# Both layers of an MLP block beside the attention of the next batch, with loads reordered and a shorter way for the first decay rows

## The chip, the cores and the metric

The kernel runs on one core of one Trainium2 chip. The metric is the time of one execution in device microseconds (us). Before the change the median was 400.74 us over 3 runs (398.77 to 401.0); a fourth joined later, so the result below has 400.87. A profile is one execution with the hardware profiler on. Its span, from the first instruction to the last, is 1.7 us shorter than the time of that same execution (397.3 of 399.01 us before the change), so spans are compared with spans and times with times.

Engine names in profile lines: PE is the matrix engine, PEld its weight loads, DVE the vector engine, ACT the scalar engine, POOL the GpSimd engine, SP the engine that issues most of the transfers. A name with a q (SPq, ACTq) is an engine's queue of instructions such as DMA issues. A line of the timeline gives start and length in us, engine, source line, operation, tiles, shape and count; a bracket at its end gives how long the engine stood idle before it, and what ended that. The tiles: `qkf` and `v_f` are loaded q, k and v, `t` the cast q and k, `pT` and `pX` transposes, `S` a bank of scores, `Pm` their exponentials, `ph` and `po` the banks of layers 1 and 2, `trl` and `gT` the two steps of the gate, `osb` the output on its way to DRAM. SBUF is the memory on the core that the engines work in; PSUM is the memory that PE writes to, in banks. The granted clock is the share of its full clock that PE was given.

## The reference

Eight batches of eight heads, 576 tokens, head size 64. A causal attention with a decay is followed by a two-layer MLP with a gate:

```python
s_pos = np.maximum(s, 0.0)
cum   = np.cumsum(s_pos, axis=-1)
bias  = -(cum[:, :, :, None] - cum[:, :, None, :])
scores = np.where(causal, -1e9, q @ k.T / 8 + np.minimum(bias, 0.0))
x = softmax(scores) @ v                      # (4608, 512) after the heads are put side by side
h = x @ w_in                                 # layer 1, 512 -> 2048
g = h * np.clip(h + 3.0, 0.0, 6.0) / 6.0     # the gate
out = g @ w_out                              # layer 2, 2048 -> 512
```

## The kernel before

Heads are handled in 32 pairs, four pairs to a batch. A pair's q and k are loaded in f32, cast to f16 on POOL, and transposed on PE in two groups of 5 and 4 tiles; DVE copies each group from PSUM into `qT` and `kT`. Rows 64 to 67 of these hold the decay, so that one matmul gives score plus bias. They come from a scratch tensor in DRAM:

```python
nc.scalar.dma_start(out=kaug_dram..., in_=kaug)     # store all heads' decay rows
nc.scalar.dma_start(out=qaug_dram..., in_=qaug)
load_aug(0, nc.scalar)                              # reload those of pairs 0 and 1
load_aug(1, nc.scalar)
```

The scores of one head are four PSUM banks (tag S, three buffers). ACT makes the exponentials, POOL cuts off the upper triangle, PE multiplies by v (`attend`) and transposes the result into `xT`:

```python
def att_tasks(p):                                   # pair p; the number is the task's cost in the weave
    tasks = [(loads, 0)]                            # aug of p+2, q,k,v of p+3, weights.get(p)
    tasks += 4 x (scores_bank(2p, bi), 400)
    tasks += (attend(2p-1), 1200)
    tasks += (transpose_group(p+1, 0), 640)         # the two groups stand apart
    tasks += 4 x (scores_bank(2p+1, bi), 400)
    tasks += (casts, 0)                             # cast_v(p+1), cast_qk(p+2)
    tasks += (x_transpose(p-1), 640)
    tasks += (transpose_group(p+1, 1), 512)
    tasks += (attend(2p), 1200)
```

*(The additions stand here for the loops and appends of the source.)*

`weave` lays the attention tasks of one batch between the MLP tasks of a block, in proportion to these costs. The MLP works in nine blocks of 512 tokens. One task of layer 1 is four matmuls into a bank, then ACT and DVE make the gate; one task of layer 2 is four of the sixteen matmuls of an output tile:

```python
def m1(n, f):
    ph = psum.tile([128, 512], F32, tag="M", bufs=2)
    ... 4 matmuls ...
    nc.scalar.activation(out=trl, in_=ph, func=AF.Relu, bias=bias3[:, 0:1], scale=1.0)
    nc.vector.scalar_tensor_tensor(out=gT[n][:, f, :], in0=trl, scalar=6.0, in1=ph, ...)

def m2(n, t4, part):
    if part == 0:
        pouts[n, t4] = psum.tile([128, 512], F32, tag="Y", bufs=1, ...)   # one bank
    ... 4 matmuls; after part 3: DVE scales into osb, sync stores it ...

weave(att_of[1], m1_tasks(0))
for n in range(NBLK - 1):                           # layer 1 of n+1 with layer 2 of n, interleaved
    att = att_of[n + 2] if n + 2 < B else []
    weave(att, merged(m1_tasks(n + 1), m2_tasks(n)))
for task in m2_tasks(NBLK - 1):                     # the last layer 2, alone
    task()
```

The weights come in eight chunks on POOL's queue, issued with the loads of pairs 1 to 5: `w_in` with pairs 1 to 3 (two chunks with pair 2), `w_out` with pairs 4 and 5 (two each).

The softmax here doesn't subtract the row's maximum and nothing guards it: scores larger than these inputs give would overflow.

## Time and profile before

| | before |
|---|---|
| median of timed runs | 400.74 us |
| span of the profile | 397.3 us |
| first matmul of layer 1 | 45.0 us |
| end of the stretch with layer 1 of block 0 and batch 1 | 82.6 us |
| a block with both layers and one batch | 39.8 us |
| the last layer 2 with its store | 20.7 us |

### The profile page before, as it was taken

The numbers are of one execution on the slowest core, as the hardware profiler recorded it, in microseconds if no ns is written. First come the engines' busy times: TensorE is split into PE (matmuls) and PEld (weight loads), VectorE is DVE, ScalarE is ACT, GpSimd is POOL, SyncE is SP. The second block draws the span as 40 slices with busy tenths as digits, with TensorE's granted clock in tenths as the row PEclk, the third lists the DMA queues.
The fourth block names the chain that finished last, engine by engine and source line by source line (L and its number), as shares of the span: only waits on it lengthen the run. The fifth ranks groups of instructions, "written<-read, shape, count | busy, mean of one in ns | idle before, by whom it ended". The sixth has DMA issues, their size and how long they took to land.

```text
span 397.3 us, 8194 instructions
## 1 busy us (share of the span) xinstructions
PE 366.4 (92%) x3040; PEld 209.7 (53%) x3040; DVE 227.2 (57%) x417; ACT 210.8 (53%) x406; POOL 140.3 (35%) x333
## 2 busy tenths in 40 slices
PE   7584776899999999999999999999999999999985
PEld 3363443555555555555555555555555544444432
DVE  4574372756666666666666666666665564454511
ACT  6364473755555566666666555555556633443400
POOL 3394825544444444444444444444443200000000
PEclk9999698999999999999999999999999999999999
DMA  9999999955555555554555455455100001010111
GB/s 176 201 213 205 185 208 178 194 108 118 116 118 118 119 117 118 119 117 117 118 118 118 108 126 114 109 126 116 38 28 27 28 26 54 26 53 28 49 58 54
DMA packets 123512, 43.40 MB, mean 109 GB/s; under 512 B 114192, under 2 KB 118672, under 8 KB 123472
## 3 DMA queue, kind: packets, MB, share of 16 engines
q1 hardware_dynamic: 117456, 37.89, 43.9%
q0 software_dynamic: 4224, 4.19, 6.4%
q10 hardware_dynamic: 1792, 0.79, 0.9%
q8 instruction: 24, 0.39, 0.4%
q14 instruction: 16, 0.13, 0.1%
HBM read 37.32 MB, written 9.73 MB: 118 GB/s over the span
## 4 chain that ended last, share of the span: by engine, by line
PE 80%; DMA 10%; POOL 4%; DVE 3%; ACT 2%; issue 1%; SPq 0%; POOLq 0%; ACTq 0%
PE po L335 31%; PE ph L317 29%; PE S L211 8%; DMA qkf<-in_k_dram 7%; PE O L260 6%; PE pT L171 3%; PE pX L285 2%; POOL Pm L224 2%; POOL t L153 1%; DMA kaug_scratch<-kaug 1%; DMA kT<-kaug_scratch 1%; ACT trl L325 1%; ACT Pm L219 1%; DMA s_sb<-in_s_dram 1%; DVE osb L344 1%; DVE gT L326 1%
## 5 line engine op out<-in xcount | busy, mean ns | idle before, releaser
L326 DVE SCALAR_TENSOR_TENSOR gT<-trl,ph 128x512 f16<-128x512 f32 x144 | 98.8, 687 | 114.7 <-ACT trl L325 114.5
L219 ACT ACTIVATE Pm<-S 128x384 f16<-128x384 f32 (+2 forms) x256 | 113.7, 506 | 80.3 <-PE S L211 72.5
L317 PE MATMUL ph<-xT,w_in_sb 128*128 128x512 f16 x576 | 147.4, 381 | 0.0
L335 PE MATMUL po<-w_out_sb,gT 128*128 128x512 f16 x576 | 144.4, 379 | 2.3 <-DVE osb L344 2.3
L325 ACT ACTIVATE trl<-ph,bias 128x512 f32<-128x512 f32 x144 | 99.6, 692 | 82.8 <-PE ph L317 81.0
L224 POOL TENSOR_SCALAR_AFFINE_SELECT Pm<-Pm 128x128 f16<-128x128 f16 (+2 forms) x256 | 78.8, 313 | 154.6 <-ACT Pm L219 144.8
L211 PE MATMUL S<-qT,kT 128*128 128x320 f16 (+4 forms) x448 | 71.4, 265 | 8.0 <-DMA kT<-kaug_scratch 3.0
L335 PEld LDWEIGHTS <-gT 128*128 128x128 f16 x576 | 51.2, 98 | 49.4 <-issue 3.2
L317 PEld LDWEIGHTS <-w_in_sb 128*128 128x128 f16 x576 | 52.2, 98 | 44.5 <-issue 1.1
L211 PEld LDWEIGHTS <-kT 128*128 128x128 f16 x448 | 42.1, 99 | 35.3 <-issue 4.9
L153 POOL CAST t<-qkf 128x1152 f16<-128x1152 f32 x32 | 36.7, 1147 | 21.4 <-DMA qkf<-in_k_dram 21.4
L260 PEld LDWEIGHTS <-Pm 128*128 128x128 f16 x960 | 37.4, 97 | 7.8 <-POOL Pm L224 1.6
L260 PE MATMUL O<-v_h,Pm 128*128 128x65 f16 x960 | 40.8, 193 | 0.5 <-POOL Pm L224 0.5
L171 PE MATMUL pT<-ident,t 128*128 128x128 f16 x288 | 26.8, 222 | 13.5 <-POOL t L153 12.9
L181 DVE COPY qT<-pT 64x640 f16<-64x640 f16 x64 | 28.3, 442 | 17.7 <-PE pT L171 17.6
L171 PEld LDWEIGHTS <-t 128*128 128x128 f16 x288 | 21.1, 99 | 28.1 <-POOL t L153 14.6
L344 DVE TENSOR_SCALAR osb<-po 128x512 f32<-128x512 f32 x36 | 24.8, 690 | 13.8 <-PE po L335 13.2
L182 DVE COPY kT<-pT 64x640 f16<-64x640 f16 x64 | 29.4, 459 | 0.9
L272 DVE TENSOR_TENSOR xs<-O,r 128x640 f16<-128x640 f32 x32 | 26.4, 824 | 1.1
L159 POOL CAST v_h<-v_f 128x640 f16<-128x640 f32 x28 | 20.1, 718 | 0.0
L285 PEld LDWEIGHTS <-xs 128*128 128x128 f16 x160 | 11.8, 99 | 10.9 <-issue 6.2
L293 DVE COPY xT<-pX 128x576 f16<-128x576 f16 x32 | 14.5, 453 | 1.7 <-PE pX L285 1.5
(29 smaller groups left out, 56.6 us busy)
## 6 DMA issues: line engine op xcount, KB each, us to landing
qkf<-in_q_dram SPq DMA_DIRECT2D x32, 288.0 KB
qkf<-in_k_dram SPq DMA_DIRECT2D x32, 288.0 KB
out_dram<-osb SPq DMA_DIRECT2D x36, 256.0 KB
v_f<-in_v_dram SPq DMA_DIRECT2D x62, 128.0 KB
w_in_sb<-in_moe_w_in_dram POOLq DMA_DIRECT2D x4, 512.0 KB, 8.1
w_out_sb<-in_moe_w_out_dram POOLq DMA_DIRECT2D x4, 512.0 KB, 10.1
v_f<-in_v_dram SPq DMA_DIRECT2D x31, 32.0 KB
kT<-kaug_scratch SPq DMA_DIRECT2D x30, 6.8 KB
```

The costliest lines, as they stand in the source:

```text
L153: nc.gpsimd.tensor_copy(out=t, in_=qk_f.pop(p))
L171: nc.tensor.matmul(out=pT[:, (t - t0) * 128:(t - t0 + 1) * 128], lhsT=src[:, t, :, :], rhs=ident, is_transpose=True, start=(t == t0), stop ...
L182: nc.vector.tensor_copy(out=kT[0:64, sl, c0:c0 + n], in_=pT[64:128, 0:n])
L211: nc.tensor.matmul(out=S[:, c:c + hi - lo], lhsT=kT[:, sl, off + 128 * kt:off + 128 * (kt + 1)], rhs=qT[:, sl, off + lo:off + hi], start=( ...
L219: nc.scalar.activation(out=P[:, p0:p0 + n], in_=S[:, 0:n], func=AF.Exp, scale=0.125, bias=0.0)
L224: nc.gpsimd.affine_select(out=view, in_=view, pattern=pattern, compare_op=ALU.is_ge, fill=0.0, base=0, channel_multiplier=-1,)
L260: nc.tensor.matmul(out=O[:, hh, qt * VW:qt * VW + D + 1], lhsT=P[:, c:c + 128], rhs=v_h[:, sl, hh, kt, 0:D + 1], start=(qt == 0), stop=(qt ...
L317: nc.tensor.matmul(out=ph, lhsT=w_in_sb[:, kc, f * 128:(f + 1) * 128], rhs=xT[:, kc, n * 512:(n + 1) * 512], start=(kc == 0), stop=(kc == ...
L325: nc.scalar.activation(out=trl, in_=ph, func=AF.Relu, bias=bias3[:, 0:1], scale=1.0)
L326: nc.vector.scalar_tensor_tensor(out=gT[n][:, f, :], in0=trl, scalar=6.0, in1=ph, op0=ALU.min, op1=ALU.mult)
L335: nc.tensor.matmul(out=po, lhsT=gT[n][:, f, t4 * 128:(t4 + 1) * 128], rhs=w_out_sb[:, f, :], start=(f == 0), stop=(f == NF - 1),)
L344: nc.vector.tensor_scalar_mul(out=osb, in0=po, scalar1=1.0 / 6.0)
```

## The change

Five things are changed together. Both layers of block n now run in turn beside the attention of batch n+1, layer 1 with a small share of the attention and layer 2 with most of it; so block 0 is finished beside batch 1 and the last layer 2 no longer stands alone after its own layer 1. The layer-2 bank joins the banks of layer 1 (three buffers for both). From pair 4 on, both transpose groups of the next pair stand together at the end of a pair, with the cast right before `attend`. Loads and weight chunks are issued in order of need. Pair 0's decay rows go straight from SBUF to SBUF instead of through DRAM. Two small edits come along: v of pair 0 is loaded from SP's queue instead of ACT's, and PE gets fewer warm-up matmuls at the start (18 and 6 instead of 22 and 10). The diff, cut to its core:

```diff
-        ph = psum.tile([128, 512], F32, tag="M", bufs=2)
+        ph = psum.tile([128, 512], F32, tag="M", bufs=3)
...
-            pouts[n, t4] = psum.tile([128, 512], F32, tag="Y", bufs=1, name=f"po{n}_{t4}")
+            pouts[n, t4] = psum.tile([128, 512], F32, tag="M", bufs=3, name=f"po{n}_{t4}")
...
     mask_rows(0, nc.scalar.copy)
+    for r in range(2):
+        for hh in range(2):
+            nc.scalar.dma_start(
+                out=kT[64 + r:65 + r, 0, hh * SEQ:(hh + 1) * SEQ], in_=kaug[hh:hh + 1, r, :]
+            )
     nc.scalar.activation(out=qaug, in_=c8, func=AF.Copy, scale=-1.0)
-    mask_rows(1, nc.scalar.copy)
+    for hh in range(2):
+        c0, c1 = hh * SEQ, (hh + 1) * SEQ
+        nc.scalar.dma_start(out=qT[67:68, 0, c0:c1], in_=qaug[hh:hh + 1, :])
+        nc.scalar.dma_start(out=kT[66:67, 0, c0:c1], in_=kaug[hh:hh + 1, 2, :])
     ... the two stores to DRAM ...
-    load_aug(0, nc.scalar)
+    mask_rows(1, nc.scalar.copy)
     load_aug(1, nc.scalar)
...
+    loads_at = {0: [3], 1: [4]}             # pairs 5 and 6: see `late`; from pair 5 on: p + 2
+    weights_at = {1: 0, 2: 1, 3: 2, 4: 3}   # w_in chunks
...  att_tasks, for p >= 4
+            if more:
+                c.append((lambda: cast_qk(p + 1), 0))
+            c.append((lambda: attend(2 * p), 1200))
+            c.append((casts, 0))
+            if more:
+                c.append((lambda: transpose_group(p + 1, 0), 640))
+                c.append((lambda: transpose_group(p + 1, 1), 512))
...
+    def block_tasks(n, w1):                 # w1: weight of a layer-1 task against 1.0 of layer 2
+        ts = [(lambda f=f: m1(n, f), w1) for f in range(NF)]
+        ts += [(lambda t4=t4, part=part: m2(n, t4, part), 1.0 if 4 * t4 + part < 13 else 0.0) ...]
...
+    late = {                                # issued after that task of block 0
+        1: lambda: load_w_out(0),
+        4: lambda: load_w_out(1),
+        7: lambda: (load_qk(5, nc.sync), load_v(5, nc.sync), load_w_out(2)),
+        10: lambda: load_w_out(3),
+        13: lambda: (load_qk(6, nc.sync), load_v(6, nc.sync)),
+    }
...
-    weave(att_of[1], m1_tasks(0))
-    for n in range(NBLK - 1):
-        att = att_of[n + 2] if n + 2 < B else []
-        weave(att, merged(m1_tasks(n + 1), m2_tasks(n)))
-    for task in m2_tasks(NBLK - 1):
-        task()
+    weave(att_of[1], first)
+    for n in range(1, NBLK):
+        weave(att_of[n + 1] if n + 1 < B else [], block_tasks(n, 0.3))
```

More of the change, by code (lines that the diff above doesn't have):

```diff
@@ L161, in banks @@
     def banks(early):
-        return dict(tag="M", bufs=2) if early else dict(tag="S", bufs=3)
+        return dict(tag="M", bufs=3) if early else dict(tag="S", bufs=3)
     def transpose_group(p, g):
@@ L349, with keep_warm @@
     nc.vector.memset(bias3, 3.0)
+    def keep_warm(n):
+        pw = psum.tile([128, 512], F32, tag="M", bufs=3, name="pw")
+        for i in range(n):
+            nc.tensor.matmul(
+                out=pw, lhsT=warm[:, 0:128], rhs=warm, start=(i == 0), stop=(i == n - 1)
+            )
     load_qk(0, nc.sync)
-    load_v(0, nc.scalar)
     load_qk(1, nc.sync)
+    load_v(0, nc.sync)
     load_v(1, nc.sync)
@@ L358 @@
     mask_rows(0, nc.scalar.copy)
+    for r in range(2):
+        for hh in range(2):
+            nc.scalar.dma_start(
+                out=kT[64 + r:65 + r, 0, hh * SEQ:(hh + 1) * SEQ], in_=kaug[hh:hh + 1, r, :]
+            )
     nc.scalar.activation(out=qaug, in_=c8, func=AF.Copy, scale=-1.0)
-    mask_rows(1, nc.scalar.copy)
+    for hh in range(2):
+        c0, c1 = hh * SEQ, (hh + 1) * SEQ
+        nc.scalar.dma_start(out=qT[67:68, 0, c0:c1], in_=qaug[hh:hh + 1, :])
+        nc.scalar.dma_start(out=kT[66:67, 0, c0:c1], in_=kaug[hh:hh + 1, 2, :])
     nc.scalar.dma_start(
@@ L364, with loads @@
     nc.scalar.dma_start(out=qaug_dram.rearrange("r (h t) -> h (r t)", h=NH), in_=qaug)
-    load_aug(0, nc.scalar)
+    mask_rows(1, nc.scalar.copy)
     load_aug(1, nc.scalar)
-    def keep_warm(n):
-        pw = psum.tile([128, 512], F32, tag="M", bufs=2, name="pw")
-        for i in range(n):
-            nc.tensor.matmul(
-                out=pw, lhsT=warm[:, 0:128], rhs=warm, start=(i == 0), stop=(i == n - 1)
-            )
-    weights = {
-        1: [(load_w_in, 0)],
-        2: [(load_w_in, 1), (load_w_in, 2)],
-        3: [(load_w_in, 3)],
-        4: [(load_w_out, 0), (load_w_out, 1)],
-        5: [(load_w_out, 2), (load_w_out, 3)],
-    }
-    def att_tasks(p):
-        def loads():
-            if p + 2 < NP:
-                load_aug(p + 2, nc.sync)
-            if p + 3 < NP:
-                load_qk(p + 3, nc.sync)
-                load_v(p + 3, nc.sync)
-            for load, c in weights.get(p, []):
-                load(c)
-        more = p + 1 < NP
-        tasks = [(loads, 0)]
-        for bi in range(4):
-            tasks.append((lambda bi=bi: scores_bank(2 * p, bi), 400))
-        if p > 0:
-            tasks.append((lambda: attend(2 * p - 1), 1200))
-        if more:
-            tasks.append((lambda: transpose_group(p + 1, 0), 640))
-        for bi in range(4):
-            tasks.append((lambda bi=bi: scores_bank(2 * p + 1, bi), 400))
+    loads_at = {0: [3], 1: [4]}
+    weights_at = {1: 0, 2: 1, 3: 2, 4: 3}
+    def loads(p):
+        if p + 2 < NP:
+            load_aug(p + 2, nc.sync)
+        for m in loads_at.get(p, [p + 2] if 5 <= p < NP - 2 else []):
+            load_qk(m, nc.sync)
+            load_v(m, nc.sync)
+        if p in weights_at:
+            load_w_in(weights_at[p])
+    def att_tasks(p):
+        more = p + 1 < NP
+        early = p < 4
         def casts():
@@ L409, in casts @@
                 cast_v(p + 1)
-            if p + 2 < NP:
+            if early and p + 2 <= 4:
                 cast_qk(p + 2)
-        tasks.append((casts, 0))
+        a = [(lambda: loads(p), 0)]
+        for bi in range(4):
+            a.append((lambda bi=bi: scores_bank(2 * p, bi), 400))
         if p > 0:
-            tasks.append((lambda: x_transpose(p - 1), 640))
-        if more:
-            tasks.append((lambda: transpose_group(p + 1, 1), 512))
-        tasks.append((lambda: attend(2 * p), 1200))
-        return tasks
+            a.append((lambda: attend(2 * p - 1), 1200))
+        if early:
+            a.append((lambda: transpose_group(p + 1, 0), 640))
+        for bi in range(4):
+            a.append((lambda bi=bi: scores_bank(2 * p + 1, bi), 400))
+        if early:
+            a.append((casts, 0))
+        if p > 0:
+            a.append((lambda: x_transpose(p - 1), 640))
+        c = []
+        if early:
+            c.append((lambda: transpose_group(p + 1, 1), 512))
+            c.append((lambda: attend(2 * p), 1200))
+        else:
+            if more:
+                c.append((lambda: cast_qk(p + 1), 0))
+            c.append((lambda: attend(2 * p), 1200))
+            c.append((casts, 0))
+            if more:
+                c.append((lambda: transpose_group(p + 1, 0), 640))
+                c.append((lambda: transpose_group(p + 1, 1), 512))
+        return a, c
+    att_of = [[]]
+    for p in range(NP):
+        a, c = att_tasks(p)
+        att_of[-1] += a
+        if p % 4 == 0 and p > 0:
+            att_of.append([])
+        att_of[-1] += c
+    att_of[-1] += [(lambda: attend(NH - 1), 1200), (lambda: x_transpose(NP - 1), 640)]
     def weave(att, mlp):
         total = float(sum(c for _, c in att)) or 1.0
-        done = 0.0
-        for i, task in enumerate(mlp):
-            while att and done / total < i / len(mlp):
+        whole = float(sum(w for _, w in mlp))
+        done, due = 0.0, 0.0
+        for task, w in mlp:
+            due += w
+            while att and done / total < due / whole:
                 a, c = att.pop(0)
@@ L432, in weave @@
             a()
-    def m1_tasks(n):
-        return [lambda f=f: m1(n, f) for f in range(NF)]
-    def m2_tasks(n):
-        return [lambda t4=t4, part=part: m2(n, t4, part) for t4 in range(4) for part in range(4)]
-    def merged(a, b):
-        out_ = []
-        for t in range(4):
-            f, g = a[4 * t:4 * t + 4], b[4 * t:4 * t + 4]
-            out_ += [g[0], g[1], f[0], g[2], f[1], g[3], f[2], f[3]]
-        return out_
-    keep_warm(22)
+    def block_tasks(n, w1):
+        ts = [(lambda f=f: m1(n, f), w1) for f in range(NF)]
+        ts += [
+            (lambda t4=t4, part=part: m2(n, t4, part), 1.0 if 4 * t4 + part < 13 else 0.0)
+            for t4 in range(4) for part in range(4)
+        ]
+        return ts
+    keep_warm(18)
     cast_qk(0)
@@ L454 @@
     cast_qk(1)
-    keep_warm(10)
-    att_all = []
-    cut = []
-    for b in range(B):
-        for p in range(4 * b, 4 * b + 4):
-            att_all += att_tasks(p)
-            if p % 4 == 0:
-                cut.append(len(att_all) - 2)
-    att_all += [(lambda: attend(NH - 1), 1200), (lambda: x_transpose(NP - 1), 640)]
-    cut.append(len(att_all))
-    att_of = [att_all[cut[b]:cut[b + 1]] for b in range(B)]
-    for task, _ in att_all[:cut[1]]:
-        task()
-    weave(att_of[1], m1_tasks(0))
-    for n in range(NBLK - 1):
-        att = att_of[n + 2] if n + 2 < B else []
-        weave(att, merged(m1_tasks(n + 1), m2_tasks(n)))
-    for task in m2_tasks(NBLK - 1):
-        task()
+    keep_warm(6)
+    for task, _ in att_of[0]:
+        task()
+    first = block_tasks(0, 0.2)
+    first[:8] = [(task, 0.0) for task, _ in first[:8]]
+    late = {
[5 more added lines that the diff above has]
+    }
+    for i, what in late.items():
+        task, w = first[i]
+        first[i] = ((lambda task=task, what=what: (task(), what())), w)
+    weave(att_of[1], first)
+    for n in range(1, NBLK):
+        weave(att_of[n + 1] if n + 1 < B else [], block_tasks(n, 0.3))
 _INS = ['q', 'k', 'v', 's', 'moe_w_in', 'moe_w_out']
```

## The prediction

> **What bounds the kernel now.** I read three views in this order: the busy time in stretches of the span, the chain that ended last, and the timeline where the two said something. First the stretches (start:end, their sum, busy us of PE, PEld, DVE, ACT, POOL with instruction counts, granted clock, DMA share, GB/s):
>
> ```profile
> 30.00:40.00 10.00, 4.51 (x74) 3.66 (x73) 4.70 (x10) 4.63 (x12) 3.77 (x10) 0.95 1.17 206
> 40.00:50.00 10.00, 7.37 (x70) 4.93 (x71) 3.93 (x9) 4.84 (x10) 8.86 (x18) 0.71 1.05 183
> 50.00:60.00 10.00, 7.22 (x76) 4.47 (x74) 7.06 (x13) 6.78 (x14) 2.26 (x7) 1.00 1.21 208
> ...
> 100.00:120.00 20.00, 20.00 (x182) 11.85 (x181) 12.73 (x25) 12.04 (x24) 8.48 (x20) 1.00 0.54 116
> ```
>
> There are two regimes. Until about 80 us the DMA engines are full (share 1.0, near 200 GB/s) and PE has gaps. From 90 us to 380 us PE is busy for the whole of every stretch and nothing else is near full. The chain names what PE waited for early on (start, length):
>
> ```profile
> 29.03 11.91 DMA qkf<-in_k_dram
> ...
> 45.22 16.20 DMA qkf<-in_k_dram
> ```
>
> These are the loads of pairs 5 and 7, stretched because the weight chunks move beside them.
>
> PE prices, as distances between starts in the timeline: a 128x512 matmul 0.216 us (8 in 1.73); the 15 of one attend 0.47; transposes of a pair 0.28 + 0.23; the x transposes 0.28; four score banks of a head 0.38 + 0.31. A pair of heads is then 2x0.69 + 2x0.47 + 0.79 = 3.11 us, a batch of four pairs 12.4, one layer of a block 64x0.216 = 13.8. A block with both layers and a batch is 27.6 + 12.4 = 40.0 us. It holds 128 + 4x58 = 360 matmuls, and at 182 in 20 us the trace gives 39.6: the steady state is at PE's own rate, without waits. So before = 45.0 (first layer-1 matmul) + 37.6 (layer 1 of block 0 beside batch 1, until 82.6) + 6x39.8 + 2x27.6 (no attention left) + 16.6 (the last layer 2) + 4.1 (last eviction and store) = 397.3.
>
> Two weak places remain. The 37.6 us stage holds only 13.8 + 12.4 = 26.2 us of PE work. At the end, each 16 matmuls of the last layer 2 wait for the one output bank:
>
> ```profile
> 380.75 3.61 PE L335 MATMUL po<-w_out_sb,gT 128*128 128x512 f16 x16 [0.78 <-DVE osb L344]
> 385.15 3.61 PE L335 MATMUL po<-w_out_sb,gT 128*128 128x512 f16 x16 [0.78 <-DVE osb L344]
> ```
>
> They start 4.40 us apart instead of 3.46, three times: 2.8 us.
>
> **What the Trainium skill says.** "TensorE: Matmul & The Clock Gate", section "Step-by-step: what each phase is for": matmuls stay in program order, only weight loads are pulled ahead. So one score matmul that waits for a copy holds all layer-2 work behind it; the timeline below agrees (0.71 us). Its section "Wait — 56ns, not 53.3ns?" gives 215.7 ns per warm N = 512 matmul; the trace has 216. "DMA: Bandwidth & Descriptors", section "Queues, rings and completion order", says each DMA engine round-robins between queue rows per packet. The weights' queue has 4224 packets in 6.4% of the time and the loads' queue 117456 in 43.9%, so a weight packet takes four times as long and I expect weights to get more than half while both run; the stretched loads agree.
>
> **What the change does, part by part.**
>
> *End.* Layer 2 of block 8 gets three banks: +0.93x3 = 2.8 us gained. Block 0 now does its layer 2 (13.8 us) beside batch 1, where PE was 11 us short of work, so if nothing else gave way 13.8 us of the tail would move into a hole.
>
> *Start.* Pair 0's decay rows take one hop. Before, the store landed at 12.3 us and the reload at 16.0. But ACT, which must make the exps, now also copies the masks of slot 1 and issues the reload of pair 1 after its store has landed, before its first exp. The store itself now waits in its semaphore lane for a load of v (the built program's order of waits). I put that at 10.5 + 4.2 = 14.7, so the first exp at about 15.5 against 16.4: 1 us, not 3.5. Then pairs 1 to 4 at before's 4.5 us each. The second half of pair 4 no longer waits for pair 5's transposes (7 us idle before 42.26). But pair 4's own q and k are issued only after pair 0's scores and share the DMA with weight chunks. First layer-1 matmul at 36 us against 45.0: 9 us gained.
>
> *Block 0.* Its transposes of pair 6 are PE's next wait. The built order sends pair 7's loads ahead of pair 6's. By then pairs 0 to 5, 7 and q, k of 6 plus all eight weight chunks must have come, the same bytes that before had at 61.5 us. So that step stands at about 63 us, however early PE began. After it are left 11 parts of layer 2 plus some 65% of a batch: 11x0.86 + 8 and the last three parts, 20 us, plus waits of 3: block 0 ends at 86 us.
>
> *Steady blocks 1 to 5.* Here is the new cost. In before, two layers were mixed: eight groups of four MLP matmuls per pair. Now 16 groups of layer 1 carry 27% of the batch and layer 2 carries 73%: four groups per pair. The one stretch of before with that density is layer 1 of block 0. Once its loads are in, its pattern repeats from a ph at 66.94 to one at 74.70: 7.76 us for 3.46 + 3.11 = 6.57 of PE work, so 1.2 us lost per pair. What loses it:
>
> ```profile
> 72.62 0.69 DVE L326 SCALAR_TENSOR_TENSOR gT<-trl,ph 128x512 f16<-128x512 f32 x1 [0.49 <-ACT trl L325]
> ...
> 73.22 0.48 DVE L181 COPY qT<-pT 64x640 f16<-64x640 f16 x1
> 73.71 0.49 DVE L182 COPY kT<-pT 64x640 f16<-64x640 f16 x1
> ...
> 74.26 0.30 PE L211 MATMUL S<-qT,kT 128*128 128x320 f16 x1 [0.71 <-DVE kT L182]
> ```
>
> PE needs the copies, and they queue behind the gating op. I walked the built PE order of one block with these delays (matmul end to trl 0.21, trl 0.69, gT 0.6, copies 0.49 + 0.49 then 0.41 + 0.43, cast 1.15, exp 0.26 after its bank, then about 0.42 each):
> - End of layer 1, then pT9, four po, seven S: the copies come 0.21 + 0.69 + 0.03 + 0.61 + 0.98 + 0.05 = 2.57 us after the last ph, PE has 0.51 + 0.86 to do: 1.2 us. The third bank then waits for the slot of the second pT: 0.5.
> - Pair's last scores, pX, four po, attend, pT5: the q,k cast is now placed after the last selects of that pair, ready 2.5 us later, PE has 1.6: 0.9.
> - pT5, po, pT4, six S: copies 0.15, slot of pT4 0.55.
> - Seven S in a row with three banks: 0.4.
> - pT9 directly before S: 1.26 - 0.23 = 1.0.
> - In layer 1, pT4, ph, S behind gT: 0.3.
>
> The sum is 5.0 us a block, against 3.5 by the 1.2 us per pair for the 2.9 pairs in layer 2. I take 4.6: 44.6 a block, 223 for five. Block 6 has fewer transposes: 41.5. Layer-1 groups without attention cycle three banks in 0.86 + 0.21 + 0.72 + 0.69 + 0.05 = 2.53 us, under 3x0.864 = 2.59: no wait, so blocks 7 and 8 stay 27.6 each.
>
> *Sum:* 86 + 223 + 41.5 + 55.2 + 4.2 = 410 us span. The timed runs of before lie 1.7 to 3.7 above its span, so 412. Waits that I stack one by one partly hide each other; I say 410.
>
> **Rivals.** (1) *PE stays full.* If the evictions keep up, the steady blocks stay at 39.9 and block 0 ends at 80: 80 + 200 + 40 + 55 + 4 = 379 span, 381 timed. For it: no engine but PE is above 64% in the steady state; the weights by layer look chosen by trial. Against it: the 0.71 us waits at the same density. (2) *Only half the waits show*, 2.3 us a block: about 398, no change. (3) *The loads are the worse wait*: weight chunks take four fifths of the DMA from 30 to 50 us, pair 5 comes at 48 and pair 6 at 66, PE idles long enough to lose clock (0.71 at 40 to 50 us in before): 416. (4) *DMA hardly matters*, block 0 ends by 79 us, with steady waits of 4.6: 403.
>
> **Range and chances.** Block 0's end is uncertain by 5 us and the per-block wait by 1.3 us x6 = 8; together about 9 around 410, longer downward since (1) has arguments. 396 to 419. Under 392.7 (2% faster) needs nearly rival 1: 0.14. Between 392.7 and 408.8: 0.34. Above: 0.52.
>
> **What would show it.** Right: PE below 9.2 of 10 from 100 to 280 us, with waits of S for kT copies, of pT for the cast t, and of S for Pm adding up to 4 to 5 us per block; about 160 matmuls per 20 us; first ph near 36; no wait on osb at the end; stores of block 0 over by about 87. Wrong: PE at 10.00 in the steady stretches (rival 1), or a first exp near 13 us, or no qkf wait after 45 us.

## More of the kernel before

The page of the kernel before starts with the busy time of each engine, and then cuts the span into 40 slices of about 10 us with a digit for the tenths of each that an engine was busy:

```profile
PE 366.4 (92%) x3040; PEld 209.7 (53%) x3040; DVE 227.2 (57%) x417; ACT 210.8 (53%) x406; POOL 140.3 (35%) x333
...
PE   7584776899999999999999999999999999999985
...
DMA  9999999955555555554555455455100001010111
```

One looks for the row of nines. It stands in the DMA line for the first eight slices and in the PE line from the ninth on. The kernel has two stages with different limits, and a change is judged in the stage that it touches. The stretch of the steady blocks alone, by the view of stretches (columns: start:end, sum, then busy us and count of PE, PEld, DVE, ACT, POOL, then granted clock, DMA share, GB/s), is:

```profile
100.00:280.00 180.00, 180.00 (x1618) 106.94 (x1617) 114.73 (x216) 108.14 (x216) 76.27 (x180) 1.00 0.54 117
```

PE is busy in all 180 us and works off 1618 matmuls. The next engine, DVE, is at 114.73/180 = 64%.

## The result and the profile after

| | before | after |
|---|---|---|
| median of timed runs (lowest to highest) | 400.87 (398.77 to 402.29) | 418.37 (417.77 to 418.61) |
| ratio, 95% interval | | 1.0439 (1.0391 to 1.0486) |
| span of the profile | 397.3 | 416.1 |

The changed kernel is 4.4% slower. A ratio here is the mean time of one kernel's runs over that of the other's of the same rounds, so it is not quite the ratio of the medians quoted.

The page of the changed kernel, in the same two parts as shown for before:

```profile
PE   7388958799889998899789988999889999999996
...
DMA  9899996824455543742265445654274100102002
```

The row of nines in the PE line is broken by eights and sevens until slice 30, which ends at 312 us, just before block 6; behind it the row is whole up to the last slice. So the steady blocks no longer run at PE's rate. The view of stretches for the same 180 us says it in numbers:

```profile
100.00:280.00 180.00, 164.61 (x1438) 94.46 (x1436) 103.97 (x190) 97.62 (x192) 67.45 (x159) 1.00 0.48 104
```

PE is busy for 164.61 of 180 us instead of all, and does 1438 matmuls instead of 1618. The clock is full and no other engine rose: PE waits. The starts of the blocks in the timeline give the account by stage:

| stage | before | after | after minus before |
|---|---|---|---|
| until block 0 (both layers) and batch 1 are done | 82.6 + 13.8 for the layer 2 that comes later = 96.4 | 90.27 | -6.1 |
| five blocks with a batch | 5 x 39.8 = 199.0 | 5 x 45.23 = 226.2 | +27.2 |
| block 6 with the last batch | 39.8 | 40.45 | +0.65 |
| the 256 matmuls of two blocks without attention | 55.2 | 55.24 | 0 |
| bank waits, last eviction and store | 2.8 + 4.1 = 6.9 | 4.0 | -2.9 |
| sum | 397.3 | 416.1 | +18.8 |

*(The last layer 2 of before took 16.6 us, of which 13.8 are counted in the first row because the other kernel does that amount of work there.)*

**The end.** The timeline of the changed kernel shows the last layer 2 as one run of 64 matmuls (columns: start, length, engine, line, operation, tiles, shape, count):

```profile
398.33 13.98 PE L335 MATMUL po<-w_out_sb,gT 128*128 128x512 f16 x64
```

No bracket with a wait follows, and the run is not cut into groups of 16. The three waits of 0.9 us are gone.

**The steady blocks.** In the timeline, the end of layer 1 in block 1 reads:

```profile
108.91 0.69 DVE L326 SCALAR_TENSOR_TENSOR gT<-trl,ph 128x512 f16<-128x512 f32 x1 [0.18 <-ACT trl L325]
109.51 0.47 DVE L181 COPY qT<-pT 64x640 f16<-64x640 f16 x1
110.00 0.49 DVE L182 COPY kT<-pT 64x640 f16<-64x640 f16 x1
...
110.55 0.56 PE L211 MATMUL S<-qT,kT 128*128 128x256 f16 x4 [1.03 <-DVE kT L182]
...
111.53 0.46 PE L211 MATMUL S<-qT,kT 128*128 128x320 f16 x3 [0.42 <-ACT Pm L219]
```

The transposes that these two copies empty had started on PE at 107.99 us. Their copies stand on DVE behind the last gate of layer 1, and the first scores on PE stand behind the copies, 1.19 us later than the work before them allows. Right after, the third bank of scores (the last line) waits for one of the three PSUM slots that scores and transposes share; the profile names ACT's exponential as what came last. Summed over the span, the view of waits (engine, line, what it waited for: us in total, times, longest) has in the changed kernel:

```profile
PE pT L171 <- POOL t L153: 12.2, 10, 5.5
PE S L211 <- ACT Pm L219: 12.2, 28, 3.5
PE S L211 <- DVE kT L182: 11.9, 18, 1.0
```

Over the span copies, score slots and casts each hold PE for some 12 us. A part of the first two lines lies before the steady blocks, with the single waits of 5.5 us (at 63.33 us) and 3.5 us (at 17.87 us).

**The start.** ACT's queue and work in the timeline before the change:

```profile
8.83 0.57 ACTq L364 DMA_DIRECT2D qaug_scratch<-qaug  x1
...
16.43 0.98 ACT L219 ACTIVATE Pm<-S 128x384 f16<-128x384 f32 x2 [6.79 <-PE S L211]
```

and after it:

```profile
6.09 2.53 ACTq L370 DMA_DIRECT2D kT<-kaug  x4
8.67 0.68 ACT L373 ACTIVATE qaug<-c 64x576 f16<-64x576 f32 x1 [2.08 <-issue]
9.39 0.50 ACTq L376 DMA_DIRECT2D qT<-qaug  x1
10.09 0.50 ACTq L377 DMA_DIRECT2D kT<-kaug  x1
10.79 0.56 ACTq L376 DMA_DIRECT2D qT<-qaug  x1
11.40 0.60 ACTq L377 DMA_DIRECT2D kT<-kaug  x1
12.04 0.65 ACTq L378 DMA_DIRECT2D kaug_scratch<-kaug  x1
12.73 0.74 ACTq L381 DMA_DIRECT2D qaug_scratch<-qaug  x1
13.51 1.15 ACT L111 COPY kT<-amask 64x1152 f16<-64x1152 f16 x1 [4.15 <-DMA v_f<-in_v_dram]
...
17.33 1.69 ACT L219 ACTIVATE Pm<-S 128x384 f16<-128x384 f32 x4 [1.62 <-DMA qaug_scratch<-qaug]
```

The bracket of the mask copy blames a load of v for 4.15 us, but the lines above it show what filled that time: six issues, one every 0.6 to 0.8 us. Four of them are row copies of pair 0, and four more row copies had already held ACT for 2.53 us from 6.09 on. The store of the decay rows is the last of the six; it starts at 12.73 us where before's had started at 8.83. Pair 1's reload waits for it to land, 4.23 us later by the chain of waits, and ACT's first exponential comes only after that reload is issued: at 17.33 us, against 16.43 before. The short way for pair 0 put the long way of pair 1 behind eight issues that were not there before. The first matmul of layer 1 starts at 37.91 us.

**Block 0.** The timeline of SP's queue, POOL and PE around the next long wait:

```profile
43.07 10.26 SPq L136 DMA_DIRECT2D v_f<-in_v_dram  x2
...
62.13 1.14 POOL L153 CAST t<-qkf 128x1152 f16<-128x1152 f32 x1 [5.03 <-DMA qkf<-in_k_dram]
...
63.33 1.14 PE L171 MATMUL pT<-ident,t 128*128 128x128 f16 x9 [5.47 <-POOL t L153]
```

PE stands 5.47 us for pair 6's transposes, because the cast waits for pair 6's k, which lands at 62.0 us. It was issued at 55.08: the queue had been held from 43.07 to 53.33 by two halves of v of pair 7, a pair that is needed later. After this idle time the granted clock falls (0.83 in the stretch from 60 to 70 us). The nine transposes and the four matmuls behind them take 2.64 us where full speed needs 1.37.

### The profile page after: what moved, and what is told of

Its sections match the earlier page's. It is cut to its first block, busy times and chain, and to the rows that moved or that the text cites. A ratio compares the mean times of both kernels' runs of the same rounds, so it can differ in the third digit from the quotient of the medians.

```text
span 416.1 us, 8186 instructions
## 1 busy us (share of the span) xinstructions
PE 370.0 (89%) x3032; PEld 207.8 (50%) x3032; DVE 231.6 (56%) x417; ACT 213.5 (51%) x406; POOL 140.9 (34%) x333
## 4 chain that ended last, share of the span: by engine, by line
PE 74%; DVE 6%; DMA 6%; ACT 6%; POOL 3%; issue 2%; ACTq 1%; SPq 0%; POOLq 0%
PE ph L317 28%; PE po L335 26%; PE S L211 10%; PE O L260 6%; ACT Pm L219 4%; DMA qkf<-in_k_dram 3%; PE pT L171 3%; POOL t L153 2%; DVE kT L182 2%; DVE qT L181 2%; ACT trl L325 2%; DVE gT L326 2%; PE pX L285 2%; DMA qaug_scratch<-qaug 1%; DMA kT<-kaug 1%
## 5 line engine op out<-in xcount | busy, mean ns | idle before, releaser
L219 ACT ACTIVATE Pm<-S 128x384 f16<-128x384 f32 (+2 forms) x256 | 115.5, 504 | 100.4 <-PE S L211 97.5
L335 PE MATMUL po<-w_out_sb,gT 128*128 128x512 f16 x576 | 140.3, 381 | 0.0
L317 PE MATMUL ph<-xT,w_in_sb 128*128 128x512 f16 x576 | 137.4, 379 | 0.0
L211 PE MATMUL S<-qT,kT 128*128 128x320 f16 (+4 forms) x448 | 70.3, 264 | 27.2 <-ACT Pm L219 12.2
L335 PEld LDWEIGHTS <-gT 128*128 128x128 f16 x576 | 52.8, 98 | 51.0 <-issue 3.4
L211 PEld LDWEIGHTS <-kT 128*128 128x128 f16 x448 | 38.6, 99 | 52.0 <-DVE kT L182 20.6
L260 PEld LDWEIGHTS <-Pm 128*128 128x128 f16 x960 | 38.4, 98 | 10.3 <-POOL Pm L224 1.1
L171 PE MATMUL pT<-ident,t 128*128 128x128 f16 x288 | 25.3, 225 | 12.3 <-POOL t L153 12.2
L171 PEld LDWEIGHTS <-t 128*128 128x128 f16 x288 | 19.4, 100 | 26.7 <-POOL t L153 16.7
L270 DVE RECIPROCAL r<-O 128x10 f32<-128x10 f32 x32 | 7.0, 219 | 35.4 <-PE O L260 35.3
```

The lines of the kernel that those rows point to most:

```text
L171: nc.tensor.matmul(out=pT[:, (t - t0) * 128:(t - t0 + 1) * 128], lhsT=src[:, t, :, :], rhs=ident, is_transpose=True, start=(t == t0), stop ...
L211: nc.tensor.matmul(out=S[:, c:c + hi - lo], lhsT=kT[:, sl, off + 128 * kt:off + 128 * (kt + 1)], rhs=qT[:, sl, off + lo:off + hi], start=( ...
L219: nc.scalar.activation(out=P[:, p0:p0 + n], in_=S[:, 0:n], func=AF.Exp, scale=0.125, bias=0.0)
L260: nc.tensor.matmul(out=O[:, hh, qt * VW:qt * VW + D + 1], lhsT=P[:, c:c + 128], rhs=v_h[:, sl, hh, kt, 0:D + 1], start=(qt == 0), stop=(qt ...
L317: nc.tensor.matmul(out=ph, lhsT=w_in_sb[:, kc, f * 128:(f + 1) * 128], rhs=xT[:, kc, n * 512:(n + 1) * 512], start=(kc == 0), stop=(kc == ...
L335: nc.tensor.matmul(out=po, lhsT=gT[n][:, f, t4 * 128:(t4 + 1) * 128], rhs=w_out_sb[:, f, :], start=(f == 0), stop=(f == NF - 1),)
```

## The experiments

Each was built from the changed kernel (a_) or from the kernel before (b_). All gave correct results. The first four ran beside before at 400.16 us median; a_order, a_start, b_end and b_loads beside 400.08 (same chip); the last four on another chip beside 398.65. Ratios are against before.

### a_cast: only the cast earlier

```diff
+        sooner = p >= 8 and more
         a = [(lambda: loads(p), 0)]
+        if sooner:
+            a.append((lambda: cast_qk(p + 1), 0))
...
-            if more:
+            if more and not sooner:
                 c.append((lambda: cast_qk(p + 1), 0))
```

PE's order does not change, only the place of the cast on POOL.

> Changed kernel, with the q,k cast of pair p+1 put ahead of pair p's selects from pair 8 on; the order on PE is untouched. Theory (PE waits in its order for copies, casts and score banks): only the wait of pT for the cast goes, 0.7 us in each of blocks 1 to 5 and 0.8 us at the end of block 0, so about 4 us less, near 414; a steady block takes 44.5 us instead of 45.2. Rival (the density of attention in layer 2 is the cause, whatever waits there are): another wait takes its place, 418.

Measured: 413.53 us, ratio 1.0358 (1.0304 to 1.0412), span 411.8: less than the changed kernel by 4.8 us of median, 4.3 of span and 3.2 by the ratios. In the view of waits the casts fall from 12.2 us in 10 times to 8.0 in 5, which by the timeline all lie in the first 81 us, while scores behind `kT` copies stay at 11.9 us in 18 times. Block 1 takes 44.32 us instead of 45.23. So the late cast cost about 0.9 us a steady block, 3 to 5 us in all, and the waits for copies are independent of it.

### a_trans: the transpose groups apart again

```diff
+        apart = p >= 8 and more          # and the cast as in a_cast
...
-        if early:
+        if early or apart:
             a.append((lambda: transpose_group(p + 1, 0), 640))
...
+        elif apart:
+            c.append((casts, 0))
+            c.append((lambda: transpose_group(p + 1, 1), 512))
+            c.append((lambda: attend(2 * p), 1200))
```

This gives PE, from pair 8 on, the order of tasks of the kernel before (the casts are placed otherwise, as in a_cast), and leaves everything else of the change as it is, the two layers one after the other included.

> Changed kernel, from pair 8 on with the cast early and the two transpose groups of pair p+1 set apart again: one between the two heads' scores, one before the attend; the shares of 27% and 73% of attention by layer stay. Theory of the order: a steady block falls from 45.2 us to about 41 (what stays is 0.4 us for each run of seven score matmuls), blocks 1 to 5 give 21 us and the end of block 0 some 2, so 395 us, under before. Rival (density): blocks keep 44 to 45 us, 412 to 418. Rival (the loads of block 0 are the whole loss): 418.

Measured: 396.41 us, ratio 0.9914 (0.9859 to 0.997), span 394.6. A steady block takes 41.08 us (from 132.81 to 173.89) instead of 45.23. The stretch and the waits of this run:

```profile
100.00:280.00 180.00, 177.30 (x1578) 105.05 (x1576) 115.77 (x216) 107.90 (x214) 73.55 (x175) 1.00 0.51 109
```

```profile
PE S L211 <- ACT Pm L219: 9.6, 20, 3.9
PE pT L171 <- POOL t L153: 9.2, 6, 5.1
...
PE S L211 <- DVE kT L182: 1.2, 2, 0.9
```

PE is back at 177.30 of 180 us, and the waits for `kT` copies fell from 18 to 2. So 5 x 4.15 = 20.8 of the 27.2 us lost in the steady blocks came from where the cast and the two transpose groups stand in a pair, and not from the layers being separated. The spans differ by 21.5 us. The other 1.3 us a block stay; waits for score slots, 0.25 and 0.42 us by their brackets in that block, are a good part of them.

### a_even: attention spread evenly over both layers

```diff
-        weave(att_of[n + 1] if n + 1 < B else [], block_tasks(n, 0.3))
+        weave(att_of[n + 1] if n + 1 < B else [], block_tasks(n, 1.0))
```

> Changed kernel, with the attention shared evenly over layer 1 and the first 13 parts of layer 2 in blocks 1 to 6 (weight 1.0 for 0.3); the order inside the attention stays. Rival (density, most with layer 2): this undoes it, a steady block falls to 40 to 41 us, 394 to 398 in all. Theory of the order: each T9 or T5,T4 that stands one MLP group before its scores still waits, now behind the gating op too, 1.2 us three times a block; a steady block takes 43.5 to 44.5 us, 411 to 414.

Measured: 412.87 us, ratio 1.0331 (1.0282 to 1.0379), span 410.6; block 1 takes 44.22 us. PE is busy 168.06 of the 180 us. The waits of scores for `kT` copies do not fall (14.6 us in 17 times), those for score slots do (6.0 in 10 times, from 12.2 in 28). The weight of 0.3 therefore costs something while the groups stand together (1.0 us a block, 5.5 us of span), but a lower density of attention does not remove the waits for the copies.

### a_both: a_trans and a_even together

The edit is the sum of the two diffs above.

> Both edits: transposes apart and cast early from pair 8 on, and attention shared evenly over the layers in blocks 1 to 6. Theory of the order: 40.2 to 40.6 us a steady block, hardly better than the transposes apart alone, 391 to 394. Rival (density): the whole gain comes from the even share, so this equals the even one.

Measured: 395.68 us, ratio 0.9905 (0.9858 to 0.9951), span 394.0, a steady block 41.23 us (131.81 to 173.04). This missed what I expected of a block and of the total (391 to 394): evening out adds nothing once the groups stand apart. A wait comes up in layer 1 that a_trans does not have, in the timeline of this run:

```profile
139.57 0.33 PE L211 MATMUL S<-qT,kT 128*128 128x320 f16 x2 [0.77 <-ACT Pm L219]
```

In ACT's order a `trl` of layer 1, started at 138.45 us, stands before the exponentials whose slots are wanted; they start at 139.04. With more scores in layer 1 the exponentials meet more of these. So the density of attention in layer 2 is not the main cause of the loss, and the prediction's picture of it (four MLP groups per pair) is refuted as such, though each wait that it named existed.

### a_order: pair 6 loaded before pair 7

```diff
-        7: lambda: (load_qk(5, nc.sync), load_v(5, nc.sync), load_w_out(2)),
+        7: lambda: (load_qk(5, nc.sync), load_v(5, nc.sync), load_qk(6, nc.sync), load_v(6, nc.sync), load_w_out(2)),
         10: lambda: load_w_out(3),
-        13: lambda: (load_qk(6, nc.sync), load_v(6, nc.sync)),
```

> Changed kernel, with the loads of pair 6 issued ahead of those of pair 7. Theory (block 0 stands at pair 6's transposes at 63.3 us because pair 7's 0.88 MB went first): q and k of pair 6 land 4 to 4.5 us earlier, the 5.5 us gap of PE shrinks to about 1, the lower clock after it goes too, so 412 to 413. Rival (all eight weight chunks have to come first, so the order of the two pairs is nothing): no change, 418.

Measured: 412.58 us, ratio 1.0323 (1.0266 to 1.038), span 411.7. Block 0 is over at 85.89 instead of 90.27 us. The timeline of this run at the same place:

```profile
59.98 0.68 PE L171 MATMUL pT<-ident,t 128*128 128x128 f16 x9 [1.71 <-POOL t L153]
```

The wait is 1.71 instead of 5.47 us, and the nine transposes take 0.68 instead of 1.14 us: the clock no longer falls. The k of pair 6 is now issued at 42.65 us and takes 16.08 us by the chain of waits, to land 3.3 us earlier than in the changed kernel (58.73 instead of 62.00). Its place in the queue was worth that much; the rest of its time it spent beside other transfers on full DMA engines (208 GB/s from 42 to 58 us).

### a_start: an earlier first exponential

```diff
-    mask_rows(1, nc.scalar.copy)
-    load_aug(1, nc.scalar)
...
     def loads(p):
+        if p == 0:
+            load_aug(1, nc.sync)
...
+    mask_rows(1, nc.vector.tensor_copy)
     mask_rows(2, nc.vector.tensor_copy)
```

> Changed kernel, with ACT freed at the start: mask rows of slot 1 copied by DVE and the reload of pair 1's decay rows issued by SP, where ACT held its first exp until 17.3 us. Theory: the first exp comes near 14.3 us (when the last of pair 0's rows lands) and the first layer-1 matmul 1 to 2 us earlier than 37.9, but block 0 stands for pair 6's load as before, so the time stays at 417 to 418. Rival (the start chain sets the end): 3 us less, 415.

Measured: 420.6 us, ratio 1.0524 (1.0475 to 1.0573), span 419.2. This missed both expectations: slower than the changed kernel, by 2.2 us of median and 3.1 of span. The first exponential came at 13.56 us, 3.8 us earlier, as meant, and yet the first matmul of layer 1 at 41.41, 3.5 us later. In the timeline of this run PE stands here:

```profile
34.55 0.45 PE L171 MATMUL pT<-ident,t 128*128 128x128 f16 x5 [3.12 <-POOL t L153]
```

The cast waited for pair 4's k, which took 10.04 us from its issue at 23.26 by the chain of waits, against 7.58 in the changed kernel. The first weight chunk is issued with pair 1's scores, and so went out at 19.54 us instead of 22.32, in front of that load. A stage that starts earlier issues its prefetches earlier, too. The load explains 2.6 of the 3.5 us: these transposes start at 34.55 instead of 31.91. The rest lies behind them, where the granted clock fell to 0.57 in the stretch from 36 to 40 us.

### a_startw: the same, with every weight chunk one step later

```diff
-    weights_at = {1: 0, 2: 1, 3: 2, 4: 3}
+    weights_at = {2: 0, 3: 1, 4: 2}
...
-        1: lambda: load_w_out(0),
-        4: lambda: load_w_out(1),
-        7: lambda: (load_qk(5, nc.sync), load_v(5, nc.sync), load_w_out(2)),
-        10: lambda: load_w_out(3),
+        1: lambda: load_w_in(3),
+        4: lambda: load_w_out(0),
+        7: lambda: (load_qk(5, nc.sync), load_v(5, nc.sync), load_w_out(1)),
+        10: lambda: (load_w_out(2), load_w_out(3)),
```

*(And the edit of a_start.)*

> The freed start, with every weight chunk asked for one step later (layer 1's from pair 2 on). The freed start alone lost 2.3 us, though its first exp came at 13.6 us: its first weight chunk went out at 19.5 us instead of 22.3, ahead of pair 4's q and k, whose k then took 10 us. Theory (what sets the first layer-1 matmul is pair 4's load, stretched by weights): that matmul comes at 35 to 37 us instead of 41.4; the end of block 0 still stands for pair 6, so 416 to 419 in all. Rival (DVE's extra mask copies or the late reload of pair 1 cost it): it stays at 40 to 41.

Measured: 420.03 us, ratio 1.0543 (1.0502 to 1.0584), span 418.4. The first matmul of layer 1 came at 36.65 us, as expected; that confirms the chunk as the reason of the miss in a_start. But the total was just above the expected range, and the timeline shows where it went:

```profile
64.38 1.14 PE L171 MATMUL pT<-ident,t 128*128 128x128 f16 x9 [7.78 <-POOL t L153]
```

The whole gain of the start, and some more, is lost in a wait for pair 6, whose k was again issued behind the load of pair 7 (at 56.28 us). Block 0 was over at 92.50 us. An earlier start is worth nothing while that load is placed so.

### a_fix: all repairs of the changed kernel together

The edit is the sum of a_trans, a_order, and a_startw (pair 6 in `late[7]`, 13 removed).

> All mends of the changed kernel together: transposes apart and cast early from pair 8 on, pair 6 ahead of pair 7, freed start, weights one step later. Theory: 41.1 us for each of blocks 1 to 5, block 0 over at 81 to 83 instead of 90.3, so 389 to 391. Rival (the waits hide each other): near the transposes alone, 396.

Measured: 390.49 us, ratio 0.9775 (0.9716 to 0.9834), span 386.7. One of its four runs (394.46 us) lies over 1.5% above the fastest, counts as slow, and is left out of the ratio; the median of the three others is 388.39 us. The timeline of this run has at pair 6:

```profile
57.34 0.68 PE L171 MATMUL pT<-ident,t 128*128 128x128 f16 x9 [0.40 <-POOL t L153]
```

Now the early start reaches the end of block 0 (83.8 us instead of 90.27, a little later than the 81 to 83 expected), and the next block takes 41.06 us. As an account of the causes this closes: with the groups apart, pair 6 in its turn and the start freed, 416.1 of span becomes 386.7. The steady blocks still take 1.3 us more than the 39.8 of the kernel before.

### b_end: only the bank of the last layer 2

```diff
-            pouts[n, t4] = psum.tile([128, 512], F32, tag="Y", bufs=1, name=f"po{n}_{t4}")
+            two = dict(tag="M", bufs=2) if n == NBLK - 1 and t4 % 2 else dict(tag="Y", bufs=1)
+            pouts[n, t4] = psum.tile([128, 512], F32, name=f"po{n}_{t4}", **two)
```

> Kernel before, with only the last block's layer 2 alternating between its own bank and one of layer 1's two. Theory: the three gaps of 0.9 us at the end go, 2.8 us less, ratio 0.993. Rival (the eviction and store of the end hide it): no change.

Measured: 396.61 us, ratio 0.9927 (0.9882 to 0.9971), span 393.7. The four tiles of the last layer 2 run as one group of 64 matmuls over 13.98 us without a gap. The size of the end's gain is the 2.8 us worked out in the prediction, within what the interval resolves (0.3 to 1.2% of 400 us, that is 1 to 5 us).

### b_loads: only the weights later

```diff
     weights = {
-        1: [(load_w_in, 0)],
-        2: [(load_w_in, 1), (load_w_in, 2)],
-        3: [(load_w_in, 3)],
-        4: [(load_w_out, 0), (load_w_out, 1)],
-        5: [(load_w_out, 2), (load_w_out, 3)],
+        2: [(load_w_in, 0)],
+        3: [(load_w_in, 1)],
+        4: [(load_w_in, 2)],
+        5: [(load_w_in, 3)],
+        6: [(load_w_out, 0), (load_w_out, 1)],
+        7: [(load_w_out, 2)],
+        8: [(load_w_out, 3)],
     }
```

> Kernel before, with only the weight chunks asked for later: layer 1's four at pairs 2 to 5 and layer 2's four at pairs 6 to 8, so that q, k, v come first. Theory (the stage until 82.6 us is held by loads of pairs stretched beside weights): the first layer-1 matmul comes at about 37 us, that stage ends at 69 to 73 us, steady blocks stay at 39.8, 386 to 391 in all. Rival (the DMA engines have the same bytes to move, so the stage ends where it did): 398 to 401.

Measured: 391.53 us, ratio 0.9803 (0.9737 to 0.987), span 389.2. The first matmul of layer 1 comes at 38.50 us instead of 45.0, the stage with batch 1 ends at 74.4 instead of 82.6, and the steady blocks still have PE at 180.00 of 180 us. The first matmul, the end of the stage and the total all come a little later than expected (37, 69 to 73 and at most 391 us), and the verdict at 2% is unclear. Eight microseconds were to be had in the start of the kernel before without touching its order of work. The chain of waits of this run still holds two loads, so the stage is not free of them:

```profile
34.68 9.46 DMA qkf<-in_k_dram
...
49.18 13.15 DMA qkf<-in_k_dram
```

### b_best: b_end and b_loads together

The edit is the sum of the two diffs above.

> Kernel before with later weights and the alternating bank at the end: the two gains add, 391.5 - 2.8 = 388 to 389, ratio 0.972. If the later weights had already hidden part of the end, 391.

Measured: 385.29 us, ratio 0.9685 (0.9642 to 0.9728), span 382.8: 3.2% faster than before, and so faster than both kernels, and than the 388 to 389 us expected. It is about 2 us better than its parts together (0.9927 x 0.9803 = 0.9731). Its own second load took 10.21 us where b_loads' took 13.15, with the same code up to there, so part of this is how the transfers fell in that run on that chip. The stretch shows that the steady state was left alone:

```profile
100.00:280.00 180.00, 180.00 (x1616) 106.88 (x1615) 113.91 (x215) 107.06 (x216) 75.50 (x179) 1.00 0.51 112
```

### b_rows: only the start section of the change

The edit takes the lines from `load_qk(0)` to `load_aug(1)` of the changed kernel (pair 0's decay rows from SBUF to SBUF, `load_v(0)` on sync, `mask_rows(1)` after the stores) into the kernel before.

```diff
     load_qk(0, nc.sync)
-    load_v(0, nc.scalar)
     load_qk(1, nc.sync)
+    load_v(0, nc.sync)
...  the eight row copies, as in the change
-    load_aug(0, nc.scalar)
+    mask_rows(1, nc.scalar.copy)
     load_aug(1, nc.scalar)
```

> Kernel before with only the change's start: pair 0's decay rows from SBUF to SBUF, its store, masks and reload order, v of pair 0 on SP. Theory: ACT makes its first exp near 17.3 us instead of 16.4 and the stage stands for loads anyway, so no change within 0.5%: 399 to 402. Rival (one hop less is worth its 3.5 us): 397.

Measured: 400.55 us, ratio 1.005 (1.0016 to 1.0084), span 397.7. No gain, if anything a slight loss. ACT's first exponential is not earlier but later than before's 16.43 us, by the timeline of this run:

```profile
18.02 1.36 ACT L219 ACTIVATE Pm<-S 128x384 f16<-128x384 f32 x3 [2.26 <-DMA qaug_scratch<-qaug]
```

It stands behind the same row of issues, store and reload as in the changed kernel. And the first matmul of layer 1, at 46.81 us, stands for pair 5's load anyway, so a gain of a microsecond in front of it would hardly have arrived.

## Why the prediction was right or wrong

The prediction said 410 us, more likely slower than not; measured were 418.4. The direction and the main mechanism held, and the size was short by 8; the measured time lies close to the upper end of the stated range (396 to 419). On the spans the account by its own terms is:

| term of the sum | said | measured | too low by |
|---|---|---|---|
| block 0 over | 86 | 90.27 | 4.3 |
| five blocks | 5 x 44.6 = 223 | 5 x 45.23 = 226.2 | 3.2 |
| block 6 | 41.5 | 40.45 | -1.05 |
| blocks 7, 8 and the end | 55.2 + 4.2 | 55.24 + 4.0 | -0.2 |
| span | 410 | 416.1 | 6.1 |

The profile's span and the median of the timed runs differ by 2.3 us, inside the 1.7 to 3.7 that the prediction used. It had worked out 412 for the timed runs and then said 410, and those 2 us, with 0.3 of this difference, are the rest of the 8.4. The largest error is that of block 0.

**The end: right.** No wait for the output bank is left in the changed kernel, b_end gives the gain alone, and the term was 2.8 us.

**The steady blocks: the mechanism right, the size 0.6 us per block too small.** The signs that the prediction set for this part are met: PE at 164.61/180 = 9.15 tenths, 1438/9 = 160 matmuls per 20 us, waits for copies, cast and slots of 5.2 us per block (said were 4 to 5). The list had added up to 5.0; block 1 has, by the distances between starts on PE:

| wait of block 1 | listed | measured |
|---|---|---|
| scores behind the gate and the copies | 1.2 + 0.5 | 1.19 + 0.60 |
| late cast | 0.9 | 0.85 |
| second group and seven scores in a row | 0.15 + 0.55 + 0.4 | 0.16 + 0.60 + 0.41 |
| group of nine directly before scores | 1.0 | 0.06 + 1.02 |
| in layer 1 | 0.3 | 0.34 |
| sum | 5.0 | 5.23 |

The step that failed is the shading: 5.0 was lowered to 4.6 because a looser estimate gave 3.5, and the total by 2 us more because "waits that I stack one by one partly hide each other". They did not. Each stands on PE's own program order, after PE has run dry, so one does not shorten another.

What the prediction blamed in general, the density of attention in layer 2, was wrong as the main cause: a_even keeps the waits for the copies at lower density and gains only 1.0 us a block, and a_trans removes nearly all of them at the old density and gains 4.15. The list itself was nearer the truth than its heading, since most of its items name the two groups in a row, or the late cast.

**Block 6: 1 us too pessimistic.** Its waits had been guessed from those of the others, with fewer transposes. No run takes them apart, so this term is only recorded.

**Block 0: the stand at 63 us right, the time after it too short.** The prediction placed PE's stand at pair 6's transposes at about 63 us, from the bytes to be moved; it ended at 63.33. That it would be there "however early PE began" was shown by a_startw, where an earlier start made it longer, and the order of pairs 7 and 6 as its reason by a_order. But 20 us of work plus 3 of waits were 20.9 plus 4.75, and 1.3 us more for the lowered clock; so the sign "stores of block 0 over by about 87" did not come. The prediction had spoken of the clock only in its third rival; the Trainium skill, "TensorE: Matmul & The Clock Gate", section "What's actually happening", says that the clock is halved after an idle window of about 3.4 us, and 5.47 us of idle time with 0.93 us for nine transposes afterwards, where 0.51 is usual, agree with it. With 1.71 us of idle time in a_order it stayed full. In a_start a wait of 3.12 us, somewhat less than the page's figure, was followed by a lowered clock too.

**The start: wrong in its size.** Said were a first exponential at 15.5 and a first layer-1 matmul at 36 us; measured 17.33 and 37.91. The prediction saw that the reload of pair 1 stands before ACT's first exponential, but started the store at 10.5 us. It started at 12.73: four row copies held ACT's queue for 2.53 us, and the six issues behind them, the store's two among them, took 4.1 us. The prediction had counted the hops saved and not the issues added. It did not matter for the end of block 0, as a_startw shows: the stage ends by a load.

**The rivals.** PE did not stay full (1), and not only half of the waits showed (2). The third, worse loads with a lowered clock, came true in part: the clock fell, and cost 1.3 us. The weights had 2.73 of the 4.0 MB that moved from 30 to 50 us, more than half, as the prediction expected from packets taken in turn, but not four fifths. The fourth, that loads hardly matter, is refuted by a_order, in which block 0 ends 4.4 us earlier.

## What to carry to other kernels

Where PE works in program order, put something else between a transpose and the matmul that reads its copy, and before rescheduling whole layers check what stands in front of that copy on the engine that makes it. Waits that PE meets one after another in its own order add up, so a walk through the built order is to be taken at its full sum. Issue loads in the order in which the bottleneck engine meets them, and when an early stage is made faster, look at which prefetches move forward with it: here the gain of the start was lost once to a weight chunk that moved forward (a_start), and once to a load that stood in the wrong place (a_startw).

## What the Trainium skill lacked or had wrong

- "TensorE: Matmul & The Clock Gate", section "Back-to-back issue gap", states a sustained spacing in real kernels of about 131 ns for N = 512 and 81 ns for N = 128, and calls the isolated formula too high at large N. Here 64 pairs of weight load and matmul with N = 512 took 13.81 us from start to start of the next run, 216 ns each, and five transposes with N = 128 took 0.28 us, 56 ns each. In this kernel the isolated formula holds in the sustained state, at both sizes.
- "DMA: Bandwidth & Descriptors", section "Issuing engines are not separate DMA queues", calls the sequencer's time for issuing a DMA "usually small relative to the DMA itself". On ACT's queue six small transfers were issued one every 0.6 to 0.8 us, 4.1 us together, as long as one of them takes to land (4.03 us), and all of it was in front of ACT's own work.
- The same page gives no case of a local transfer whose issue holds its queue for long: with the engines full, two issues of v of pair 7 occupied SP's queue for 10.26 us, and delayed the issue of pair 6 behind them; in a_order two issues of v of pair 6 occupied it for 10.25 us. What held them is not settled; the view of waits names a copy on which that load does not depend.
- Neither of these two pages gives the time from the end of one engine's work to the start of the dependent work of another. In these traces it is 0.21 us from a matmul of layer 1 to ACT, 0.26 from scores to ACT, 0.20 from a matmul to DVE, and 0.05 from a DVE copy or a POOL cast to PE. The waits are sums of these and of the operations' lengths.
